# Moving the premix of the next group behind scores and the product with v, and a second bank for the last product with v

## The chip, the cores and the metric

The kernel runs on one core of a Trainium2 chip. It is one program of 22852 instructions on five queues: TensorE (matmuls, PE in the profile, with its weight loads as PEld), VectorE (DVE), ScalarE (ACT), GpSimd (POOL) and SyncE (SP), which here only starts DMA transfers. The metric is the device time of one execution in microseconds (us). Three runs of the kernel before took 1380.95, 1381.3 and 1382.7 us; the median is 1381.3 us.

## The reference

The program is an attention layer whose heads are mixed before and after the softmax, followed by two feed-forward layers. All of it is float32.

```python
def _attn_ref(q, k, v, w_pre, w_post):            # q, k, v: 4 x 12 x 448 x 64
    scores = scale * np.matmul(q, k.transpose(0, 1, 3, 2))
    scores = np.einsum('bhij,hg->bgij', scores, w_pre)      # premix of the 12 heads
    scores = scores - np.max(scores, axis=-1, keepdims=True)
    attn = np.exp(scores)
    attn = attn / (np.sum(attn, axis=-1, keepdims=True) + 1e-09)
    attn = np.einsum('bhij,hg->bgij', attn, w_post)         # postmix
    return np.matmul(attn, v)

def _moe_ref(x, w1, w2, w3, w_out):               # x: 1792 x 768
    return ((x @ w1) * (x @ w2) @ w3) @ w_out

def _moe2_ref(x, w_in, w_out):
    h = x @ w_in
    return np.maximum(0.01 * h, h) @ w_out
```

## The kernel before, in words

The attention part takes the first third of the time, the feed-forward part the rest. Only the attention part is touched.

**Tiling.** Each of the 4 batches is cut into four chunks of query rows: three of 120 rows (`c` = 0, 1, 2) and one of 88 (`c` = 3). A chunk's scores (`qk`, line 199) go through PSUM into a tile `s`, from there by DMA to DRAM (`sdr`), and come back (`relayout`, line 243) as `sr` with the heads of ten query rows on the partitions: that is a block. Two blocks make a group. A chunk of 120 rows has six groups, the one of 88 rows five, and the last of these five holds only one block.

**One step of the loop** (line 421) works on several groups at once. In step `k`:

1. `softmax(groups[k])`: VectorE finds the row maximum `mx` from the premixed scores in PSUM (line 276), ScalarE computes `e` = exp and the sum `sm` (line 279). First block A, then block B.
2. `postmix(groups[k - 1])`: TensorE multiplies `e` of the group before by its weights `kr` (line 304), and VectorE or ScalarE copies the result out of PSUM into `ap` (line 311). Between the blocks stands `weigh(groups[k])`: GpSimd adds a small number to `sm` (line 286), VectorE takes the reciprocal `rc` (line 288), GpSimd scales the weights to `kr` (line 290).
3. `premix(k + 1)`: TensorE mixes the heads of the next group's scores into two PSUM banks `pm` (line 269), one for each block.
4. `qk`: scores of a chunk two ahead, one pair of heads a step, into two banks `pq`; the last two pairs of a chunk may share a step.
5. `av`: the product with v for the chunk before, `px` (line 324). In the first step of a chunk there is none, in the second there are two, then one a step (two in the third step of a chunk with five groups). After the third and the sixth, VectorE copies `px` to `y` (line 333).
6. Small work that the list `lows` and the generator `filler` hold: the copy of `px`, splits of q and k into two parts of float32r (lines 79 and 179; that of k for the next batch stands in the last two steps of `c` = 1 and the first four of `c` = 2), and a piece of the conversion of a feed-forward weight (lines 95 to 106), one a step and two in the third step of a chunk.

**What sets the order.** Within attention the order is written by hand: every engine's queue runs the instructions in the order in which the code above issues them. The feed-forward part behind it is ordered by a scheduler when the program is built. PSUM has eight banks: two `qa` (for `pq`), three `pm`, two `po`, one `px`. A tile takes the bank that its tag hands round, and waits until the last reader of that bank is done. With three `pm` banks, block B of group k + 1 takes the bank in which block A of group k stood, so its premix waits for the exp of that block.

**The way into the feed-forward part.** Behind the loop stand the six products with v of the last chunk. The first feed-forward matmuls (`pw`, line 517) need the first tile of a converted weight `ws`: a DMA brings `wr`, ScalarE takes the absolute value (line 95), VectorE works on it in four instructions (lines 97, 100, 103, 106), ScalarE and VectorE split the result into `ws` (lines 76 and 79).

Of the kernel before, what the change touches and what calls it, by code (L numbers as in the profile page):

```python
# [23 lines left out]
def attention_moe_kernel(ctx: ExitStack, tc, qt, kt, vt, w_pre, w_post, w1, w2, w3t, w_out, w_in2, w_out2, out):  # L24
# [15 lines left out]
    P = 128  # L40
# [5 lines left out]
    CH = qt.shape[-1]  # L46
# [25 lines left out]
    def bank(tag, shape, name):  # L72
        return ps.tile(shape, F32, tag=tag, name=name, bufs=banks[tag])
# [45 lines left out]
    def attention():  # L119
        with ExitStack() as es:  # L120
# [70 lines left out]
            def q_split(b, c):  # L191
                m = cols[c]
                qs = kv.tile([P, NPAIR, 2, CH], F32R, tag="qs", name="qs", bufs=2)
                t = qls.pop((b, c))
                qst[b, c] = qs
                hi_act(qs[:, :, 0, :m], t[:, :, :m])
                return lambda: lo_dve(qs[:, :, 1, :m], t[:, :, :m], qs[:, :, 0, :m])
# [35 lines left out]
            def evict():  # L233
                while evs:
                    evs.pop(0)()

            def flush():

                while stores:
                    dst, t = stores.pop(0)  # L240
                    nc.sync.dma_start(out=dst, in_=t)  # L241
# [20 lines left out]
            def premix(k):  # L262

                sr = srt.pop(k)
                for s, n in enumerate(groups[k]):
                    pms[n] = bank("pm", [P, S], "pm")
                    rows = slice(s * Q, s * Q + blocks[n][3] // 2 * H)
                    for g in range(2):
                        nc.tensor.matmul(  # L269
                            pms[n][g * Q:(g + 1) * Q], kpre[rows], sr[rows, g, :], start=True, stop=True  # L270
                        )

            def softmax(n):
                pm = pms.pop(n)
                mx = wk.tile([P, 1], F32, tag="mx", name="mx")
                nc.vector.tensor_reduce(out=mx, in_=pm, axis=AX.X, op=ALU.max, negate=True)  # L276
                e = wk.tile([P, S], F32, tag="e", name="e", bufs=4)
                sm = wk.tile([P, 1], F32, tag="sm", name="sm")
                ends["act"] = nc.scalar.activation(  # L279
                    out=e, in_=pm, func=ACTF.Exp, bias=mx, scale=1.0, accum_out=sm  # L280
                )
                ets[n], sms[n] = e, sm
# [30 lines left out]
            def av(b, c, p):  # L313
                c0, ni, _ = chunks[c]
                ap = apt[b, c]
                g, r = divmod(p, 3)
                if p == 0:
                    ys[b, c] = yp.tile([P, NPAIR, CH], F32, tag="y", name="y")
                if r == 0:
                    pxs[0] = bank("px", [P, 3, CH], "px")  # L320
                y, px = ys[b, c], pxs[0]
                for jc in range(NJ):
                    for e in range(2):
                        nc.tensor.matmul(  # L324
                            px[e * D:(e + 1) * D, r, :ni],
                            vst[b][:, jc, 2 * p + e, :],
                            ap[:, jc, 2 * p + e, :ni],
                            start=(jc == 0),
                            stop=(jc == NJ - 1),
                        )  # L330
                if r == 2:
                    copy = nc.scalar.copy if (b, c) == order[-1] else nc.vector.tensor_copy
                    lows.append(lambda: copy(y[:, 3 * g:3 * g + 3, :ni], px[:, :, :ni]))
                if p == NPAIR - 1:
                    later.append((scr[b][:, :, c0:c0 + ni], y[:, :, :ni]))

            pxs, later = [None], []
# [40 lines left out]
            order = [(b, c) for b in range(B) for c in range(len(chunks))]  # L378
# [6 lines left out]
            NG = len(groups)  # L385
# [35 lines left out]
            for k in range(NG + 1):  # L421
                flush()
                while later:
                    stores.append(later.pop(0))
                evict()
                if k < NG:
                    b, c, t, nt = where[k]
                    ci = order.index((b, c))
                    for n in groups[k]:
                        softmax(n)  # L430
                for i in range(2):
                    if k > 0 and i < len(groups[k - 1]):
                        postmix(groups[k - 1][i], nc.scalar.copy if i and (k == NG or t % 2) else nc.vector.tensor_copy)
                    if k < NG and i < len(groups[k]):
                        weigh(groups[k][i])
                if k + 1 < NG:
                    premix(k + 1)
                if k < NG:
                    if k + AHEAD < NG:
                        relayout(k + AHEAD)  # L440
                    if ci + QAHEAD < len(order):
                        ps = [t] if nt == NPAIR else [4, 5] if t == 4 else [t]
                        if ci == 0:
                            ps = ([], [0], [1], [2], [3], [4, 5])[t]
                        for p in ps:
                            qk(*order[ci + QAHEAD], p)
                    left = nt - t if t else 1
                    for _ in range(-(-len(todo) // left)):
                        av(*todo.pop(0))
                    if t == 0 and k > 0:  # L450
                        todo += [(*where[k - 1][:2], p) for p in range(NPAIR)]
                    if ci + QAHEAD + 1 < len(order) and t == (4 if ci == 0 or c == NC - 2 else 3):
                        lows.append(q_split(*order[ci + QAHEAD + 1]))
                    if b + 1 < B:
                        if c == NC - 3 and t >= 4:
                            lows.append(k_split(b + 1, t - 4))
                        if c == NC - 2 and t < 4:
                            lows.append(k_split(b + 1, t + 2))
                while lows:
                    lows.pop(0)()  # L460
                if k < NG:
                    if c == 0 and t == 2:
                        v_prep(b)
                    if (t == 4 or k == 0) and ci + QAHEAD + (1 if k == 0 else 2) < len(order):
                        q_load(*order[ci + QAHEAD + (1 if k == 0 else 2)])
                    if b + 1 < B and c == NC - 3 and t in (0, 1, 3):
                        k_load(b + 1, (0, 1, 3).index(t))
                    if k >= START or k == START - 5:
                        for _ in range(2 if k >= START and t == 2 else 1):
                            next(filler, None)  # L470
# [242 lines left out]
```

## Time and profile before

| | |
|---|---|
| median of three runs | 1381.3 us |
| profiled execution | 1380.92 us, span 1379.1 us |
| PE busy | 1335.9 us (97% of the span) |
| DVE busy | 879.3 us (64%) |
| ACT busy | 601.9 us (44%) |
| POOL busy | 166.2 us (12%) |
| DMA queue of SyncE | 222.73 MB, 51.9% of 16 engines' span |
| chain that ended last | PE 90%, DMA 3%, DVE 2%, SPq 2%, ACT 1% |
| first `pw` that runs without a pause | 492.54 us; from there 886.6 us to the end of the span |

Some 1.8 us of the execution lie outside the span. A matmul's end in the profile is modelled, so an engine can stand as busy although the second half of a premix waits inside such a stretch; the starts of the pieces behind each other show the wait better than the busy time. The profile counts two records for each float32 matmul, so a premix of two blocks is x8 and a postmix of two blocks x16. "Releaser" names what ended a wait.

### The profile page before, as it was taken

The page shows a single profiled execution, that of the slowest core. Times are in us where ns is not written, and L with a number is a line of the kernel's source. Part 1 is how long each engine was busy: PE and PEld are TensorE (multiplying, and loading weights), DVE is VectorE, ACT ScalarE, POOL GpSimd, SP SyncE. Part 2 cuts the span into 40 slices and gives each one's busy share as a digit, 9 for nine tenths or more (in the row PEclk, how much of TensorE's full clock was granted, in tenths as well). Part 3 has the DMA queues.
Part 4 walks back from the last instruction along what each step waited for, and adds up shares of the span by engine and source line. Part 5 has one row for each costly group of instructions (what it writes and reads, how often), then busy time and mean ns, then how long its engine had stood idle before and what let it go on. Part 6 is the DMA issues. An engine that isn't in the chain of part 4 may idle for free.

```text
span 1379.1 us, 22852 instructions
## 1 busy us (share of the span) xinstructions
PE 1335.9 (97%) x8880; PEld 1128.7 (82%) x8880; DVE 879.3 (64%) x1519; ACT 601.9 (44%) x1163; POOL 166.2 (12%) x371
## 2 busy tenths in 40 slices
PE   5899999999999989999999999999999999999998
PEld 3466666666666679999898999999898989999998
DVE  4366566566566687576347696967665358596862
ACT  4366566556564354333224452443333225453340
POOL 1233333334333300000000000000000000000000
PEclk8799999999999999999999999999999999999999
DMA  5987897797697796433133432427332233342402
GB/s 170 262 292 207 246 308 234 230 313 236 206 281 250 230 294 208 132 93 91 46 119 109 139 115 92 137 90 226 104 111 66 70 115 111 121 135 93 137 1 80
DMA packets 138859, 224.18 MB, mean 163 GB/s; under 512 B 20032, under 2 KB 120384, under 8 KB 138304
## 3 DMA queue, kind: packets, MB, share of 16 engines
q1 hardware_dynamic: 138752, 222.73, 51.9%
q8 instruction: 70, 1.15, 0.3%
q14 instruction: 37, 0.30, 0.1%
HBM read 162.86 MB, written 58.98 MB: 161 GB/s over the span
## 4 chain that ended last, share of the span: by engine, by line
PE 90%; DMA 3%; DVE 2%; SPq 2%; ACT 1%; issue 1%; POOL 1%; ACTq 0%; POOLq 0%; DVEq 0%
PE pm L579 42%; PE po L648 17%; PE po L304 9%; PE pm L269 6%; PE px L324 5%; PE pq L215 5%; PE pw L517 5%; DMA sr<-sdr 1%; SPq L260 1%; ACT e L279 1%; POOL kr L290 1%; DMA wr<-in_moe_w_dram 1%; DVE mx L276 0%; SPq L241 0%; DMA kl<-in_k_dram 0%
## 5 line engine op out<-in xcount | busy, mean ns | idle before, releaser
L579 PE MATMUL pm<-x,ws 128*128 128x512 f32 (+1 forms) x2304 | 466.8, 363 | 0.0
L579 PEld LDWEIGHTS pm<-x,ws 128*128 128x128 f32 x2304 | 417.7, 188 | 47.7
L648 PE MATMUL po<-ws,g 128*128 128x384 f32 x1344 | 234.2, 334 | 0.0
L648 PEld LDWEIGHTS po<-ws,g 128*128 128x128 f32 x1344 | 233.1, 188 | 0.0
L304 PE MATMUL po<-kr,e 128*112 128x120 f32 (+1 forms) x1440 | 176.1, 275 | 2.5 <-POOL kr L290 2.4
L304 PEld LDWEIGHTS po<-kr,e 128*112 128x112 f32 x1440 | 157.2, 179 | 23.4 <-issue 9.7
L79 DVE TENSOR_TENSOR ws<-wc,ws 128x768 fp32r<-128x768 f32 (+1 forms) x104 | 101.3, 976 | 81.5 <-ACT ws L76 81.2
L279 ACT ACTIVATE e<-pm,mx 128x448 f32<-128x448 f32 x180 | 112.6, 632 | 91.1 <-DVE mx L276 90.7
L95 ACT ACTIVATE wc<-wr 128x768 f32<-128x768 f32 (+2 forms) x120 | 104.6, 874 | 82.9 <-DVE ws L79 61.4
L76 ACT ACTIVATE ws<-wc 128x768 fp32r<-128x768 f32 (+1 forms) x104 | 89.1, 859 | 107.4 <-PE po L648 73.9
L269 PE MATMUL pm<-sr,kpre 60*64 60x448 f32 x720 | 119.4, 572 | 17.0 <-DMA sr<-s 6.9
L290 POOL TENSOR_SCALAR kr<-kpost,rc 128x120 f32<-128x120 f32 x180 | 122.9, 683 | 95.9 <-DVE rc L288 43.9
L223 ACT ACTIVATE s<-pq 120x448 f32<-120x448 f32 (+1 forms) x180 | 88.5, 540 | 101.5 <-PE pq L215 101.3
L579 PE MATMUL pm<-h,ws 128*128 128x512 f32 (+1 forms) x576 | 116.3, 363 | 0.0
L276 DVE TENSOR_REDUCE mx<-pm 128x1 f32<-128x448 f32 x180 | 103.9, 617 | 18.5 <-PE pm L269 18.4
L311 DVE COPY ap<-po 112x480 f32<-112x480 f32 (+1 forms) x136 | 88.4, 650 | 41.0 <-PE po L304 38.2
L579 PEld LDWEIGHTS pm<-h,ws 128*128 128x128 f32 x576 | 104.3, 188 | 11.7
L215 PEld LDWEIGHTS pq<-ks,qs 64*120 64x120 f32 (+1 forms) x576 | 48.4, 184 | 76.5 <-issue 55.0
L106 DVE SCALAR_TENSOR_TENSOR wc<-wr,wc 128x768 uint32<-128x768 uint32 (+2 forms) x120 | 110.0, 917 | 1.3
L103 DVE SCALAR_TENSOR_TENSOR wc<-wr,wc 128x768 uint32<-128x768 uint32 (+2 forms) x120 | 109.9, 917 | 1.2
L324 PEld LDWEIGHTS px<-ap,vs 112*64 112x64 f32 x1536 | 74.0, 136 | 31.9 <-issue 24.5
L215 PE MATMUL pq<-ks,qs 64*120 64x448 f32 (+1 forms) x576 | 89.4, 414 | 10.3 <-ACT ks L76 5.8
(51 smaller groups left out, 992.1 us busy)
## 6 DMA issues: line engine op xcount, KB each, us to landing
sr<-sdr SPq DMA_DIRECT2D x172, 210.0 KB
sdr<-s SPq DMA_DIRECT2D x36, 840.0 KB
wr<-in_moe_w_dram SPq DMA_DIRECT2D x32, 768.0 KB
wr<-in_moe_w_in_dram SPq DMA_DIRECT2D x32, 768.0 KB
wr<-in_moe_w_out_dram SPq DMA_DIRECT2D x32, 768.0 KB
wr<-in_moe_w_dram SPq DMA_DIRECT2D x8, 1024.0 KB
sdr<-s SPq DMA_DIRECT2D x12, 616.0 KB
wr<-in_moe_w_out_dram SPq DMA_DIRECT2D x16, 384.0 KB
```

What stands on the lines that cost most here:

```text
L95: nc.scalar.activation(out=cf, in_=hi.bitcast(F32), func=ACTF.Abs)
L103: lambda: nc.vector.scalar_tensor_tensor(out=c, in0=hi, scalar=0xC0000000, in1=c, op0=ALU.bitwise_and, op1=ALU.bitwise_or),
L106: lambda: nc.vector.scalar_tensor_tensor(out=c, in0=lo, scalar=29, in1=c, op0=ALU.logical_shift_right, op1=ALU.bitwise_or),
L215: nc.tensor.matmul(pq[e][:m], qst[b, c][rows, p, x, :m], kst[b, p][rows, y, :], start=(j == 0), stop=(j == 2))
L269: nc.tensor.matmul(pms[n][g * Q:(g + 1) * Q], kpre[rows], sr[rows, g, :], start=True, stop=True)
L276: nc.vector.tensor_reduce(out=mx, in_=pm, axis=AX.X, op=ALU.max, negate=True)
L279: ends["act"] = nc.scalar.activation(out=e, in_=pm, func=ACTF.Exp, bias=mx, scale=1.0, accum_out=sm)
L290: ends["pool"] = nc.gpsimd.tensor_scalar(out=kr, in0=kpost, scalar1=rc, scalar2=None, op0=ALU.mult)
L304: nc.tensor.matmul(po[:, jc].rearrange("p h (g i) -> p h g i", g=2), e[:, jc * JP:(jc + 1) * JP], kr, start=True, stop=True,)
L324: nc.tensor.matmul(px[e * D:(e + 1) * D, r, :ni], vst[b][:, jc, 2 * p + e, :], ap[:, jc, 2 * p + e, :ni], start=(jc == 0), stop=(jc == NJ ...
L579: nc.tensor.matmul(dst, wt[:, a, kk, :], x[:, kk, c, c0:c0 + w], start=(kk == 0 and j == 0), stop=(kk == kn - 1 and j == 2),)
L648: nc.tensor.matmul(po, g[:, m, a, t * P:(t + 1) * P], wts[m][:, c, 0, cs], start=(m == 0 and j == 0), stop=(m == FQ - 1 and j == 2),)
```

## The change

The call of `premix(k + 1)` moves from behind the postmix to behind the products with v, at the end of the matmuls of a step. In the last six products with v, the second three go to a bank of `qa` in place of the only `px` bank.

```diff
                 if r == 0:
-                    pxs[0] = bank("px", [P, 3, CH], "px")
+                    pxs[0] = bank("qa" if g and (b, c) == order[-1] else "px", [P, 3, CH], "px")
...
                     if k < NG and i < len(groups[k]):
                         weigh(groups[k][i])
-                if k + 1 < NG:
-                    premix(k + 1)
                 if k < NG:
...
                     if t == 0 and k > 0:
                         todo += [(*where[k - 1][:2], p) for p in range(NPAIR)]
+                    if k + 1 < NG:
+                        premix(k + 1)
                     if ci + QAHEAD + 1 < len(order) and t == (4 if ci == 0 or c == NC - 2 else 3):
```

On TensorE this is the order of one step and the start of the next, at the turn from one chunk to another (the step at the turn has no product with v). Before:

```order
L304 MATMUL po<-kr,e 112x120 x8
L269 MATMUL pm<-sr,kpre 64x448 x4
L215 MATMUL pq<-ks,qs 88x448 x6
L324 MATMUL px<-ap,vs 64x120 x8
L304 MATMUL po<-kr,e 112x120 x8
L269 MATMUL pm<-sr,kpre 64x448 x4
L215 MATMUL pq<-ks,qs 120x448 x6
L304 MATMUL po<-kr,e 112x120 x8
```

And after, at the same place:

```order
L304 MATMUL po<-kr,e 112x120 x8
L215 MATMUL pq<-ks,qs 88x448 x6
L324 MATMUL px<-ap,vs 64x120 x8
L269 MATMUL pm<-sr,kpre 64x448 x4
L304 MATMUL po<-kr,e 112x120 x8
L215 MATMUL pq<-ks,qs 120x448 x6
L269 MATMUL pm<-sr,kpre 64x448 x4
L304 MATMUL po<-kr,e 112x120 x8
```

The premix (L269) has gone from the second place of a step to the last; nothing else has changed places. Within attention VectorE, ScalarE, GpSimd and SyncE keep their order; only a few loads of SyncE for the feed-forward part, near the end of the loop, stand between other loads than before.

The scheduler of the feed-forward part deals out its first instructions anew. On VectorE, right behind the last copy of the loop, `wc_6185` and `ws_6191` belong to the first weight tile, `wc_6196` and `ws_6202` to the second. Before:

```order
L97 TENSOR_SCALAR wc_6185<-wc_6185 128x1024
L100 TENSOR_SCALAR wc_6185<-wc_6185 128x1024
L103 SCALAR_TENSOR_TENSOR wc_6185<-wr_6179,wc_6185 128x1024
L106 SCALAR_TENSOR_TENSOR wc_6185<-wr_6179,wc_6185 128x1024
L97 TENSOR_SCALAR wc_6196<-wc_6196 128x1024
L100 TENSOR_SCALAR wc_6196<-wc_6196 128x1024
L103 SCALAR_TENSOR_TENSOR wc_6196<-wr_6181,wc_6196 128x1024
L79 TENSOR_TENSOR ws_6191<-wc_6185,ws_6191 128x1024
L106 SCALAR_TENSOR_TENSOR wc_6196<-wr_6181,wc_6196 128x1024
```

And after:

```order
L97 TENSOR_SCALAR wc_6185<-wc_6185 128x1024
L100 TENSOR_SCALAR wc_6185<-wc_6185 128x1024
L103 SCALAR_TENSOR_TENSOR wc_6185<-wr_6179,wc_6185 128x1024
L97 TENSOR_SCALAR wc_6196<-wc_6196 128x1024
L106 SCALAR_TENSOR_TENSOR wc_6185<-wr_6179,wc_6185 128x1024
L100 TENSOR_SCALAR wc_6196<-wc_6196 128x1024
L103 SCALAR_TENSOR_TENSOR wc_6196<-wr_6181,wc_6196 128x1024
L106 SCALAR_TENSOR_TENSOR wc_6196<-wr_6181,wc_6196 128x1024
L79 TENSOR_TENSOR ws_6191<-wc_6185,ws_6191 128x1024
```

The whole conversion of the second tile now stands ahead of the last instruction for the first one, and its first instruction ahead of the fourth for the first tile.

On TensorE, `px_6087` and `px_6113` are the two banks of the last six products with v, `pw_6207` and `pw_6235` the halves of the first feed-forward result, `pw_6274` and `pw_6307` those of the second. Before:

```order
L324 MATMUL px_6087<-ap_5898,vs_4955 64x88 x24
L324 MATMUL px_6113<-ap_5898,vs_4955 64x88 x24
L517 MATMUL pw_6207<-wo_6170,ws_6191 128x384 x2
L517 MATMUL pw_6235<-wo_6170,ws_6191 128x384 x2
L517 MATMUL pw_6207<-wo_6170,ws_6191 128x384 x22
L517 MATMUL pw_6235<-wo_6170,ws_6191 128x384 x22
```

And after:

```order
L324 MATMUL px_6087<-ap_5898,vs_4955 64x88 x24
L324 MATMUL px_6113<-ap_5898,vs_4955 64x88 x24
L517 MATMUL pw_6207<-wo_6170,ws_6191 128x384 x2
L517 MATMUL pw_6235<-wo_6170,ws_6191 128x384 x2
L517 MATMUL pw_6274<-wo_6170,ws_6202 128x384 x2
L517 MATMUL pw_6307<-wo_6170,ws_6202 128x384 x2
L517 MATMUL pw_6207<-wo_6170,ws_6191 128x384 x22
```

Four short matmuls on the second tile now come before the long part on the first.

## Rows read from the trace of the kernel before

**Rows 1.** Stretches: us, each engine's busy time (records), granted clock, DMA share, GB/s

```profile
47.50:51.50 4.00, 3.92 (x14) 1.43 (x14) 1.25 (x2) 0.00 (x0) 0.00 (x0) 0.50 1.02 249
...
54.50:479.50 425.00, 412.75 (x4036) 280.85 (x4034) 266.07 (x622) 246.09 (x620) 159.56 (x351) 1.00 0.83 252
```

**Rows 2.** Waits of 54.5 to 479.5 us: engine, tile, releaser: us, times, longest

```profile
PE pm L269 <- ACT e L279: 4.6, 10, 0.7
...
PEld pm L269 <- ACT e L279: 20.1, 25, 1.4
...
PEld po L304 <- POOL kr L290: 6.2, 13, 1.1
```

**Rows 3.** Stretches with premix (line 269) alone: us, PE busy, PEld busy, clock, DMA

```profile
54.50:479.50 425.00, 107.34 (x696) 22.97 (x696) 1.00 0.83 252
```

**Rows 4.** Timeline of PE: start, us, line, tiles, records [wait before, releaser]

```profile
106.99 1.89 PE L304 MATMUL po<-kr,e 128*112 128x120 f32 x16
108.82 0.98 PE L269 MATMUL pm<-sr,kpre 60*64 60x448 f32 x8
109.73 0.87 PE L215 MATMUL pq<-ks,qs 64*120 64x448 f32 x6
110.53 1.04 PE L324 MATMUL px<-ap,vs 112*64 112x120 f32 x16
...
111.50 1.89 PE L304 MATMUL po<-kr,e 128*112 128x120 f32 x16
...
114.95 0.97 PE L269 MATMUL pm<-sr,kpre 60*64 60x448 f32 x4 [0.66 <-ACT e L279]
```

**Rows 5.** Timeline of VectorE before the premix that waits in rows 4

```profile
111.61 0.53 DVE L333 COPY y<-px 128x360 f32<-128x360 f32 x1 [1.52 <-PE px L324]
...
113.46 1.15 DVE L276 TENSOR_REDUCE mx<-pm 128x1 f32<-128x448 f32 x2
```

**Rows 6.** Timeline of VectorE and GpSimd, 126.5 to 132 us: one group's way to kr

```profile
127.67 1.15 DVE L276 TENSOR_REDUCE mx<-pm 128x1 f32<-128x448 f32 x2
...
129.78 0.59 POOL L290 TENSOR_SCALAR kr<-kpost,rc 128x120 f32<-128x120 f32 x1 [0.36 <-DVE rc L288]
...
131.04 0.59 POOL L290 TENSOR_SCALAR kr<-kpost,rc 128x120 f32<-128x120 f32 x1 [0.37 <-PE pq L215]
```

**Rows 7.** Timeline, 97 to 103 us: a group whose second kr is slow

```profile
97.84 1.15 DVE L276 TENSOR_REDUCE mx<-pm 128x1 f32<-128x448 f32 x2
...
100.96 0.62 DVE L179 TENSOR_TENSOR ks<-kl,ks 128x448 fp32r<-128x448 f32 x1
...
101.21 1.22 POOL L290 TENSOR_SCALAR kr<-kpost,rc 128x120 f32<-128x120 f32 x1 [0.36 <-PE pq L215]
```

**Rows 8.** Timeline of PE, steps without scores (445 us)

```profile
445.05 0.98 PE L269 MATMUL pm<-sr,kpre 60*64 60x448 f32 x8
445.96 1.04 PE L324 MATMUL px<-ap,vs 112*64 112x120 f32 x16
```

**Rows 9.** Timeline of PE at the start of the loop

```profile
47.58 2.65 PE L269 MATMUL pm<-sr,kpre 60*64 60x448 f32 x8 [5.41 <-DMA sr<-sdr]
50.16 1.47 PE L215 MATMUL pq<-ks,qs 64*120 64x448 f32 x6
51.56 3.05 PE L304 MATMUL po<-kr,e 128*112 128x120 f32 x16
```

**Rows 10.** Way into the feed-forward part: timeline, then the chain that ended last

```profile
486.67 1.15 ACT L95 ACTIVATE wc<-wr 128x1024 f32<-128x1024 f32 x1 [1.62 <-DMA wr<-in_moe_w_dram]
487.53 1.22 DVE L106 SCALAR_TENSOR_TENSOR wc<-wr,wc 128x1024 uint32<-128x1024 uint32 x1
...
489.39 0.69 DVE L100 TENSOR_SCALAR wc<-wc 128x1024 uint32<-128x1024 uint32 x1
...
489.90 0.96 PE L517 MATMUL pw<-wo,ws 128*128 128x384 f32 x4 [2.75 <-ACT ws L76]
...
492.54 68.49 PE pw L517 x380
```

## The prediction

> **What bounds the kernel now.** I read the stretches of the span first. From 54.5 to 479.5 us, the loop of the attention part, TensorE is busy 412.75 of 425.00 us at a granted clock of 1.00 (of 2.4 GHz), VectorE 266.07 us, and the 16 DMA engines are 0.83 busy [rows 1]. So TensorE sets the pace, and a change of order can give back only what TensorE stands still, which is hidden in part in stretches that count as busy. The waits say for what: the weight load of the premix waits 25 times for ScalarE's exp, 20.1 us in all, its matmuls stand idle for 4.6 us, and the weight loads of the postmix wait 13 times for `kr`, 6.2 us [rows 2]. The timeline gives the size of an undisturbed step, read from start to start: postmix 1.83, premix 0.91, scores 0.80, product with v 0.97, together 4.51 us [rows 4]. The first step of a chunk has no product with v (3.53), one without scores and product 2.73.
>
> **Why the premix waits.** The bank of its second block is free when the first exp of the step is done, and that exp waits for `mx` on VectorE. In a step behind a copy of `px`, VectorE comes to `mx` late: the copy starts at 111.61, right behind the product with v, and with the small work behind it `mx` starts at 113.46, 1.96 us into the step that began at 111.50 [rows 4, 5]. The second half of the premix then starts at 114.95 where 113.33 would have done.
>
> **The change part by part.**
>
> *The waits for the bank go.* The stretch of the loop holds 696 records of premix; that is 174 blocks in 89 premixes, of which four have one block. An undisturbed one is busy 0.98 us [rows 4], 89 of them 87.2; they are busy 107.34 [rows 3], so 20.1 us of waiting stand as busy, and 4.6 us as waits [rows 2]: 24.7 us. After the change the premix starts 0.80 to 2.6 us later in its step, at least 1.75 us behind the end of the premix before, and the bank is free 1.5 us behind `mx` (113.46 to 114.95 [rows 4, 5]). No bank is late unless `mx` is 0.25 us behind the premix in the shortest step, or 2.1 us in an ordinary one. Gain: 24.7; what a late bank would cost stands in the rivals.
>
> *The old waits for `kr` go, and others come.* Of the 6.2 us in rows 2 TensorE loses 4.3: so much are the postmixes of the loop over 1.83 each from start to start on the timeline. These waits hang on the old place of `mx`. In their place: from now on `mx` cannot start before the premix that ends a step. Call that end T. What is queued behind `mx` on VectorE (copies of `po`, reciprocals, the small work) all shifts with it, and the next postmix waits for the `kr` made from it. From `mx` to the end of the first `kr` is 127.67 to 130.37, 2.70 us, to the end of the second 131.63, 3.96 us [rows 6]. With VectorE's subtraction for k beside it the second `kr` takes 1.22 in place of 0.59, and the way 97.84 to 102.43, 4.59 us [rows 7]. I add 0.05 to the start of the postmix and see where that is later than TensorE:
>
> - An ordinary step: block A is wanted at T + 4.51, B at T + 5.42. `mx` at T + 0.11 (as the copy of `px` behind its product [rows 4, 5]) gives 2.86 and 4.12, slow 4.75. No wait.
> - Fourth steps of `c` = 2, behind copy, subtraction and two pieces of conversion: in rows 5 these take 1.85 from the copy to `mx`; the copy starts 0.11 behind the product, which now ends 0.91 before T, so `mx` is at T + 1.05 and B ready at 5.69: wait 0.27. Three times: 0.8.
> - Second steps of `c` = 2 wait for a group whose `mx` stood behind copy, subtraction and one piece (1.85 less 0.38): `mx` at T + 0.67, B ready at 5.31, wanted at 3.53 + 0.91 = 4.44: 0.87. Three times: 2.6.
> - Behind the group of one block the postmix is 0.95, so that step is only 2.66 long: A waits 0.2 and B 0.35. Three times: 1.7.
> - First steps without scores (2.73): 0.15 and 0.35. Twice: 1.0.
> - The third step of the last chunk has two products with a copy between them; VectorE reaches that copy some 0.4 later, behind the reciprocals: 0.4.
>
> New waits: 6.5. The undisturbed steps keep their time, since the four pieces are the same; on ScalarE the scores' copies now come 0.9 earlier and stand out of exp's way. Two waits stay as they are: the second of two score pairs in one step, and the product behind a copy.
>
> *The start of the loop.* The premix of 47.58 waits 5.41 us for a transfer; the scores behind it (50.16 to 51.56) move into this wait [rows 9]. That saves 1.40, at a granted clock of 0.50 [rows 1]. But the clock then has the same time to rise in as before, so the next scores may still run at the low one, 1.40 for 0.80. Gain between 0.8 and 1.4; I take 1.0.
>
> *The last product.* The wait for `px` goes, but behind it TensorE waits 2.75 us, until 489.90, for the first `ws` [rows 10]: 0, since the weight stays the later one; a part of 2.75 only if the weight came sooner. The loop's last piece of conversion, the store and loads behind it move up with the loop, so I let the entry shift with it.
>
> *The first feed-forward weight.* Line 97 for the second tile now stands ahead of line 106 for the first and waits for an absolute value that ends at 487.82, where VectorE was free at 487.53. From there line 97 takes 0.69 (as line 100), line 106 1.22; then lines 100, 103 and 106 for the second tile take 0.69, 1.22 and 1.22 (line 103 as line 106), and ScalarE's split for the short matmuls 1.15 (487.53 + 1.22 to 489.90): TensorE starts its unbroken run at about 494.0 rather than 492.54 [rows 10]. Bounds: 0 if the scheduler's order costs nothing, 2.5 if the subtraction for the first tile also stands in the way. I take 1.4, since these instructions overlap a little. From there to the end TensorE has no pause worth naming in both orders.
>
> Sum, from the profiled 1380.92: - 24.7 - 4.3 + 6.5 - 1.0 + 1.4 = **1358.8, say 1359 us**. The median of the runs shown is 0.4 above that execution, which changes nothing.
>
> **Two rules weighed.** The slow `kr` of rows 7 runs beside an instruction of VectorE with two operands from SBUF. The Trainium skill, "SBUF — State Buffer", section "Who interferes with whom", says that such an instruction and one of GpSimd that reads SBUF block each other for the whole instruction, whichever issues first. The trace agrees in kind: 1.22 against 0.59. By the rule the slow `kr` comes back wherever that subtraction is queued behind the reciprocal; were it 0.59 throughout, the waits at `c` = 2 would be 0.75 and 0 in place of 2.6 and 0.8, and the sum 1356.
>
> TensorE gets new neighbours: premix ahead of postmix, product ahead of premix. A premix takes 0.91 to the next start ahead of scores and ahead of a product with v alike [rows 4, 8]. "TensorEngine Tiling (Array Packing)" of the Trainium skill, section "Key Properties", says that each change of the tiling mode drains the engine. The number of such changes in a step is the same, so by the rule the sum stays; that some pair costs more than another no run here shows, and it is the second rival.
>
> **Rivals.**
>
> - *Fewer new waits.* VectorE's small work finds room, and the 6.5 do not come, with the start at 1.4 and the entry at 0: 1380.92 - 29.0 - 1.4 = 1350.5; half of it, 1354. For it: VectorE is busy 63% of the loop [rows 1]. Against it: its order is fixed, and the way from `mx` to `kr` is as long as before. 10%.
> - *New neighbours on TensorE cost time.* The nearest price is one weight load of a postmix, about 0.11 us (1.83 for 16 records); exposed once in each of 89 steps that is 9.8: 1368.6. The same length could as well be saved, below 0. Against it: the equal 0.91 above. 12%.
> - *Transfers come late.* The loop shortens by 22 us and the DMA share rises from 0.83 to 0.87 [rows 1]; two waits like the 5.41 at the start would bring 1370. Against it: the premix now stands later in its step, and past 54.5 no premix waits for a transfer. 4%.
> - *Slower: the way from premix to `kr` sets every step.* Premix, `mx`, exp, reciprocal, `kr`, postmix follow each other with nothing in reserve but one step. If `mx` were late by 1.05 and the second `kr` slow everywhere, some 60 ordinary steps would wait 0.27 (16) and 15 first steps 1.25 (19): 35 for 6.5, 1387. It decides against the change from about 29 us of such waits, that is from a mean lateness of `mx` of about 1 us. For it: VectorE now stands idle at the head of each step. Against it: only two steps in a chunk have the copy, one has two pieces, and the subtraction stands in six of 23 steps. 8%, of which 3% between 1378 and 1384.
>
> **How the numbers follow.** The forecast has 66%, its own range 1353 to 1366. The range 1350 to 1371 adds most of the first three rivals and leaves out the slower case and the rest. A measurement of this kernel can tell about 0.2% (2.8 us) from no change. Faster by over 0.2%: 0.66 + 0.10 + 0.12 + 0.04 less a little, 0.91. Within: 0.03. Slower: 0.06.
>
> **What would show it.** In the changed profile the wait of the premix for exp should be gone from 25 places; VectorE should wait for the premix ahead of `mx` in most steps; the waits of the postmix for `kr` should be 5 to 8 us and stand in second steps; an ordinary step should stay at 4.51; the run of `pw` should start 20 to 22 us earlier, at 470 to 473, and last as long as before. The prediction is wrong if an ordinary step is over 4.6, if postmix waits for `kr` in fourth and fifth steps throughout, or if the premix waits for `sr`.

## The result and the profile after

The changed kernel takes 1358.05 us (median of four, 1357.54 to 1358.5); the one before, run beside it, 1381.24. The ratio is 0.983, with a 95% interval of 0.9813 to 0.9847. The forecast was 1359, its range 1350 to 1371. The profiled span went from 1379.1 to 1356.7 us.

**Where the time went.** Two postmixes serve as marks in both kernels: the third of the loop and the last, which holds one block. From mark to mark each piece is measured from its start to the next start. The undisturbed lengths are 1.82 for a postmix (0.91 for one block), 0.91 for a premix and 0.76 to 1.79 for one or two products; what goes beyond them by more than 0.06 is added up as late. The last postmix, which lies outside the loop, is counted in with 0.75 in both.

| us | before | after | change | predicted |
|---|---|---|---|---|
| start of the span to the third postmix | 56.26 | 54.84 | -1.42 | -1.0 |
| premixes late | 25.44 (25 places) | 1.34 (5) | -24.10 | -24.7 |
| postmixes late | 5.06 | 6.75 | +1.69 | +1.8 |
| products late | 3.42 | 3.96 | +0.54 | +0.4 |
| third to last postmix | 423.31 | 401.54 | -21.77 | -22.5 |
| last postmix to the unbroken `pw` | 12.97 | 13.38 | +0.41 | +1.4 |
| from there to the end of the span | 886.56 | 886.94 | +0.38 | 0 |

The stretches of the span after, with the columns of [rows 1]; the third is the loop between the same times of the program:

```profile
47.50:51.50 4.00, 3.78 (x15) 1.99 (x16) 1.25 (x2) 1.18 (x3) 0.22 (x1) 0.50 1.01 265
51.50:54.50 3.00, 3.00 (x25) 2.19 (x24) 1.55 (x4) 0.74 (x4) 1.03 (x3) 0.82 1.12 255
54.50:457.00 402.50, 393.43 (x4034) 276.53 (x4027) 267.07 (x621) 243.64 (x620) 158.43 (x349) 1.00 0.87 268
```

The same loop, line 269 alone, with the columns of [rows 3]:

```profile
54.50:457.00 402.50, 87.01 (x696) 18.41 (x688) 1.00 0.87 268
```

The 89 premixes are busy 87.01 us where they were 107.34 [rows 3]; 89 undisturbed ones were reckoned at 87.2. All the waiting that stood as busy is gone. The DMA share rose to the 0.87 foreseen, without a late transfer. The waits of that stretch, with the columns of [rows 2]:

```profile
DVE mx L276 <- PE pm L269: 35.6, 35, 2.1
PEld po L304 <- POOL kr L290: 32.4, 49, 1.1
...
PE px L324 <- DVE y L333: 2.9, 4, 1.0
PE po L304 <- POOL kr L290: 2.9, 10, 0.5
```

No row "pm <- ACT e" is left. In its place VectorE waits for the premix. The second row is to be read with care: the weight loads of the postmix wait 32.4 us for `kr`, five times the 6.2 of [rows 2], but the postmixes are late by only 1.7 more in all. A weight load now gets to its wait while the premix ahead of it is still running, and only what outlasts that premix costs time. TensorE's timeline shows it (columns of [rows 4]):

```profile
97.89 1.07 PE L304 MATMUL po<-kr,e 128*112 128x120 f32 x8
99.17 1.07 PE L304 MATMUL po<-kr,e 128*112 128x120 f32 x8 [0.21 <-POOL kr L290]
100.18 0.88 PE L215 MATMUL pq<-ks,qs 64*120 64x448 f32 x6
...
103.69 1.89 PE L304 MATMUL po<-kr,e 128*112 128x120 f32 x16
105.51 0.86 PE L215 MATMUL pq<-ks,qs 64*120 64x448 f32 x6
106.30 1.04 PE L324 MATMUL px<-ap,vs 112*64 112x120 f32 x16
107.27 0.98 PE L269 MATMUL pm<-sr,kpre 60*64 60x448 f32 x8
108.19 1.89 PE L304 MATMUL po<-kr,e 128*112 128x120 f32 x16
...
112.70 2.23 PE L304 MATMUL po<-kr,e 128*112 128x120 f32 x16
114.86 0.87 PE L215 MATMUL pq<-ks,qs 64*120 64x448 f32 x6
```

The step of 103.69 takes 1.82 + 0.79 + 0.97 + 0.92 = 4.50, as before. The second step of the chunk (97.89) has 0.47 more in its postmix, the fifth (112.70 to 114.86) 0.34 more. The `kr` that the fifth step waits for comes from the `mx` of the fourth step, which starts at 108.19. VectorE between the product of 106.30 and that `mx` (columns of [rows 5]):

```profile
107.39 0.53 DVE L333 COPY y<-px 128x360 f32<-128x360 f32 x1 [0.39 <-PE px L324]
107.84 0.62 DVE L179 TENSOR_TENSOR ks<-kl,ks 128x448 fp32r<-128x448 f32 x1
...
108.76 0.56 DVE L103 SCALAR_TENSOR_TENSOR wc<-wr,wc 128x384 uint32<-128x384 uint32 x1
109.23 1.15 DVE L276 TENSOR_REDUCE mx<-pm 128x1 f32<-128x448 f32 x2
```

The premix ends at 108.19 and `mx` starts 1.04 later; the forecast said 1.05.

The start of the loop on TensorE, to be held against [rows 9]:

```profile
41.99 1.00 PE L215 MATMUL pq<-ks,qs 64*120 64x448 f32 x6
47.72 2.50 PE L269 MATMUL pm<-sr,kpre 60*64 60x448 f32 x8 [4.72 <-DMA sr<-sdr]
50.15 3.05 PE L304 MATMUL po<-kr,e 128*112 128x120 f32 x16
53.13 0.87 PE L215 MATMUL pq<-ks,qs 64*120 64x448 f32 x6
```

The scores now stand ahead of the wait for the transfer, and the next ones (53.13) already take 0.80 to the following start. That was not so in every execution. move_only, a kernel of the experiments below, has the same order on TensorE up to here; its granted clock was 0.50 until 53.7 us, in the changed kernel until 52.6, and its postmix and its next scores took longer:

```profile
49.76 3.54 PE L304 MATMUL po<-kr,e 128*112 128x120 f32 x16
53.23 1.07 PE L215 MATMUL pq<-ks,qs 64*120 64x448 f32 x6
```

Now the way into the feed-forward part, on three engines, and the first `pw` without a pause in the chain that ended last (compare [rows 10]):

```profile
459.42 1.17 ACT L95 ACTIVATE wc<-wr 128x1024 f32<-128x1024 f32 x1 [4.35 <-DMA wr<-in_moe_w_dram]
...
462.44 1.13 ACT L95 ACTIVATE wc<-wr 128x1024 f32<-128x1024 f32 x1 [1.85 <-DMA wr<-in_moe_w_dram]
463.61 0.69 DVE L97 TENSOR_SCALAR wc<-wc 128x1024 f32<-128x1024 f32 x1 [0.30 <-ACT wc L95]
464.21 1.22 DVE L106 SCALAR_TENSOR_TENSOR wc<-wr,wc 128x1024 uint32<-128x1024 uint32 x1
...
468.48 2.49 DVE L79 TENSOR_TENSOR ws<-wc,ws 128x1024 fp32r<-128x1024 f32 x2
```

```profile
469.76 68.92 PE pw L517 x380
```

Line 97 for the second tile (463.61) waits 0.30 and pushes line 106 for the first to 464.21, as the forecast said. The long run then waits for two results that come within 0.02 us of each other: the first tile's subtraction (L79, 468.48 and 1.22 long) and ScalarE's split of the second tile for the short matmuls, through which the chain that ended last goes. The first weight's absolute value starts 3.04 us behind the last postmix (456.38), where it was 4.09 behind the one of 479.57. Its piece of the chain before:

```profile
483.66 1.13 ACT wc L95
```

From that start to the unbroken `pw` it is 10.34 us, where it was 8.88.

### The profile page after: what moved, and what is told of

It is laid out like the page before. It is cut to its first block, busy times and chain, and to the rows that moved or that the text cites. A ratio compares the mean times of both kernels' runs of the same rounds, so it can differ in the third digit from the quotient of the medians.

```text
span 1356.7 us, 22900 instructions
## 1 busy us (share of the span) xinstructions
PE 1317.7 (97%) x8880; PEld 1125.8 (83%) x8880; DVE 881.0 (65%) x1519; ACT 601.0 (44%) x1163; POOL 166.0 (12%) x371
## 4 chain that ended last, share of the span: by engine, by line
PE 89%; DMA 3%; DVE 2%; SPq 2%; POOL 2%; ACT 2%; issue 1%; POOLq 0%; ACTq 0%; DVEq 0%
PE pm L579 43%; PE po L648 17%; PE po L304 9%; PE px L324 5%; PE pw L517 5%; PE pm L269 5%; PE pq L215 4%; POOL kr L290 1%; SPq L260 1%; ACT e L279 1%; DMA sr<-sdr 1%; DMA wr<-in_moe_w_dram 1%; DMA sdr<-s 1%; DVE mx L276 1%; SPq L241 0%
## 5 line engine op out<-in xcount | busy, mean ns | idle before, releaser
L304 PEld LDWEIGHTS po<-kr,e 128*112 128x112 f32 x1440 | 157.3, 179 | 72.0 <-POOL kr L290 32.4
L79 DVE TENSOR_TENSOR ws<-wc,ws 128x768 fp32r<-128x768 f32 (+1 forms) x104 | 101.6, 978 | 81.6 <-ACT ws L76 81.2
L76 ACT ACTIVATE ws<-wc 128x768 fp32r<-128x768 f32 (+1 forms) x104 | 89.3, 861 | 110.1 <-PE po L648 74.0
L269 PE MATMUL pm<-sr,kpre 60*64 60x448 f32 x720 | 99.1, 571 | 11.4 <-DMA sr<-s 6.6
L97 DVE TENSOR_SCALAR wc<-wc 128x768 f32<-128x768 f32 (+2 forms) x120 | 64.9, 541 | 50.1 <-ACT wc L95 49.9
L324 PE MATMUL px<-ap,vs 112*64 112x120 f32 (+1 forms) x1536 | 90.4, 264 | 3.6 <-DVE y L333 2.9
```

The costliest lines, as they stand in the source:

```text
L269: nc.tensor.matmul(pms[n][g * Q:(g + 1) * Q], kpre[rows], sr[rows, g, :], start=True, stop=True)
L304: nc.tensor.matmul(po[:, jc].rearrange("p h (g i) -> p h g i", g=2), e[:, jc * JP:(jc + 1) * JP], kr, start=True, stop=True,)
L324: nc.tensor.matmul(px[e * D:(e + 1) * D, r, :ni], vst[b][:, jc, 2 * p + e, :], ap[:, jc, 2 * p + e, :ni], start=(jc == 0), stop=(jc == NJ ...
```

## The experiments

Times are medians. The ratio is to the kernel before, run beside them on the same chip (medians of 1380.98, 1381.3 and 1380.95 us); old_pm2 and new_late have a single run each. "Loop" is from the third to the last postmix, "entry" from the last postmix to the unbroken `pw`, "late" as above; these columns are from one profiled execution of each kernel. What precedes the third postmix differs from execution to execution (55.2 to 57.0 us with the premix in its old place, 52.6 to 55.1 in the new one), and the entry from kernel to kernel with the order that the scheduler happens to deal out. So the loop column is the one to compare.

| kernel | us | ratio, interval | loop | premix late | postmix late | entry |
|---|---|---|---|---|---|---|
| before | 1381.2 | 1 | 423.31 | 25.44 | 5.06 | 12.97 |
| the change | 1358.05 | 0.983 (0.9813 to 0.9847) | 401.54 | 1.34 | 6.75 | 13.38 |
| move_only | 1358.25 | 0.9836 (0.9822 to 0.9849) | 401.59 | 1.37 | 6.76 | 13.00 |
| bank_only | 1378.78 | 0.9984 (0.9975 to 0.9993) | 423.28 | 25.42 | 5.07 | 10.83 |
| old_defer | 1353.09 | 0.9796 (0.9781 to 0.9811) | 395.82 | 0.00 | 3.06 | 12.79 |
| new_defer | 1356.02 | 0.982 (0.9807 to 0.9834) | 400.10 | 1.01 | 5.35 | 13.23 |
| old_pm2 | 1404.19 | one run | 448.70 | 23.81 | 32.47 | 10.56 |
| new_pm2 | 1353.28 | 0.9795 (0.9782 to 0.9808) | 397.71 | 2.41 | 5.64 | 12.44 |
| new_late | 1374.51 | one run | 421.31 | 7.00 | 19.46 | 12.49 |
| entry2 | 1353.45 | 0.9796 (0.9783 to 0.9809) | 401.56 | 1.39 | 6.64 | 9.49 |
| best_a | 1350.34 | 0.9784 (0.977 to 0.9797) | 395.78 | 0.00 | 3.06 | 11.13 |
| best_b | 1350.87 | 0.9787 (0.9774 to 0.9801) | 397.78 | 2.55 | 5.51 | 11.08 |
| best_c | 1358.63 | 0.9838 (0.9824 to 0.9851) | 403.32 | 10.61 | 3.32 | 10.64 |
| best_d | 1347.43 | 0.976 (0.9747 to 0.9773) | 395.11 | 2.27 | 3.29 | 9.48 |

### Each part alone

move_only is the changed kernel without the second bank; bank_only is the kernel before with it.

```diff
-                    pxs[0] = bank("qa" if g and (b, c) == order[-1] else "px", [P, 3, CH], "px")
+                    pxs[0] = bank("px", [P, 3, CH], "px")
```

> The changed kernel, but the last product with v keeps its one px bank: only the premix has moved. Theory (the move frees the premix from waiting for exp, and the second bank hides nothing): 1358 us, as the changed kernel, within 1 us; premix waits in the loop about 1.5 us in place of 25.5, and the first unbroken pw starts within 0.3 us of that of the changed kernel (13.4 us behind the last postmix). Rival (the second bank brings part of the gain): 1359.5 to 1361.

> The kernel before, but the last three products with v take a bank of qa; the premix stays in its old place. Theory (the second bank hides nothing): 1379.5 to 1382, with the old 25 waits of the premix for exp; only the order of the first feed-forward weights on VectorE differs by one instruction, worth about 1.2 us. Rival (the second bank brings part of the gain): 1378 or less.

The move is the whole of the gain. With one bank TensorE waits again in front of the last three products (timeline of move_only):

```profile
464.50 3.79 PE L324 MATMUL px<-ap,vs 112*64 112x88 f32 x48 [4.06 <-ACT y L333]
```

Even so the unbroken `pw` starts 13.00 us behind the last postmix with this wait and 13.38 without it. But that is not because the weight is late whatever the bank does. The chain that ended last in move_only goes through the bank: from those products to the copy of `px` on ScalarE, and from there to the split of the first weight, which stands behind that copy in ScalarE's queue:

```profile
468.34 0.02 ACT y L333
...
468.62 1.07 ACT ws L76
...
469.73 68.58 PE pw L517 x384
```

In the changed kernel that split (L76) starts 9.08 us behind the last postmix, in move_only 11.89. So two waits stand beside each other there, the one for the bank and the one for VectorE. In both kernels VectorE has the first tile's subtraction (L79) behind the whole conversion of the second tile, and starts it 12.09 us behind the last postmix even where the bank is free. Taking the one wait away leaves the other. Whether the second bank is worth something once the conversions stand in turn was not run. bank_only missed its expectation by 0.7 us. Its loop is that of before to 0.03 us; what it gains lies in the entry, 2.1 us shorter. The scheduler deals out the weight conversion differently there (6.29 us from the first absolute value to the unbroken `pw`, where it was 8.88), which led to entry2.

### Another cure for the same wait

If the premix waited because `mx` came late, then VectorE can do `mx` sooner and the premix stay where it was. old_defer is the kernel before with VectorE's small work put behind `mx` and the first reciprocal; new_defer is the same edit in the changed kernel.

```diff
+            def settle():
+                while lows:
+                    lows.pop(0)()
...
                     if k < NG and i < len(groups[k]):
                         weigh(groups[k][i])
+                    if i == 0:
+                        settle()
...
                     for _ in range(-(-len(todo) // left)):
+                        settle()
                         av(*todo.pop(0))
...
-                while lows:
-                    lows.pop(0)()
+                if k >= NG - 1:
+                    settle()
```

> The kernel before, with the premix in its old place, but VectorE does the small work at a step's end (copy of px, subtractions for q and k) only behind the row maxima and the first reciprocal of the next step, so that mx is not late. Theory (the premix waited because mx stood behind that work): 1358 to 1363 us; the 25 waits of the premix for exp fall to under 5 us. Rival (the old place itself makes the premix wait, whatever VectorE does first): 1375 to 1382.

> The changed kernel, with VectorE's small work put behind the row maxima and the first reciprocal of the next step. Theory (the 6.5 us that the postmix still waits for kr come from a late mx in some steps, and in part from a slow kr beside the subtraction for k): 1355 to 1357.5 us, postmix waits 3 to 5 us. Rival (they come from the length of the way from premix to kr alone): no change, 1358.

Both theories came out against their rivals, and old_defer went past its range: 1353.09, faster than the change itself. VectorE's timeline in it, at the step that answers to [rows 5] (it starts at 108.28) and the next one (112.79):

```profile
107.96 1.14 DVE L276 TENSOR_REDUCE mx<-pm 128x1 f32<-128x448 f32 x2
...
110.04 0.51 DVE L333 COPY y<-px 128x360 f32<-128x360 f32 x1
110.47 0.66 DVE L179 TENSOR_TENSOR ks<-kl,ks 128x448 fp32r<-128x448 f32 x1
111.24 0.16 DVE L288 RECIPROCAL rc<-sm 128x1 f32<-128x1 f32 x1
111.32 0.54 DVE L106 SCALAR_TENSOR_TENSOR wc<-wr,wc 128x384 uint32<-128x384 uint32 x1
111.78 1.15 DVE L276 TENSOR_REDUCE mx<-pm 128x1 f32<-128x448 f32 x2
```

Copy and subtraction now stand behind `mx` and fill VectorE's pause ahead of the second reciprocal. `mx` starts 0.32 ahead of its step, where it was 1.96 behind the start, and the next one 1.01 ahead of its own. No premix is late any more. Postmixes are late by 3.06, less than the 5.06 of before, since an earlier `mx` makes `kr` earlier too; in the new place `mx` cannot go ahead of the premix, and new_defer keeps 5.35 + 1.01.

### How many premix banks the two places need

```diff
-    banks = {"qa": 2, "pm": 3, "po": 2, "px": 1}
+    banks = {"qa": 2, "pm": 2, "po": 2, "px": 2}
```

old_pm2 has this in the kernel before, new_pm2 in the changed one, both with all products in the two `px` banks.

> The kernel before with two pm banks in place of three, and the bank that becomes free given to px. Theory (in its old place the premix stands right behind exp, and needs the third bank): both blocks of the premix wait for both exps, 1393 to 1402 us, premix waits 40 us or more in the loop. Rival (the third bank plays no part): 1378, the gain of the second px bank (3.4 us) alone.

> The changed kernel with two pm banks in place of three, and the bank that becomes free given to px throughout (the last product too). Theory (at a step's end the exps of the group before have been done for 1 us and more, so two banks do, but for the shortest steps, 3 to 4 us): 1355 to 1358.5 us, with the product's 3.9 us of waits for the px copy gone. Rival (the premix needs three banks wherever it stands): 1365 or more.

The waits of 54.5 to 450 us in old_pm2, and those in new_pm2:

```profile
PEld pm L269 <- ACT e L279: 41.0, 61, 1.8
PE pm L269 <- ACT e L279: 22.3, 24, 1.6
```

```profile
PEld pm L269 <- ACT e L279: 4.2, 14, 0.4
```

With one bank less the old place loses 25.4 us in the loop, and its 1404.19 lies above the 1402 expected. Not all of this is waiting. The 32.47 that the table gives as postmixes late are for the most part the pause in front of the premix behind them, since its first block now waits for exp as well. And in five stretches of the loop, 17 us together, the granted clock is 0.50, which no other kernel has there; each begins less than 1 us behind a premix in front of which TensorE had stood still for 0.96 to 1.56 us, though other pauses as long have none behind them. The first of them (the premix with its wait, then the stretch with the columns of [rows 1]):

```profile
118.58 1.58 PE L269 MATMUL pm<-sr,kpre 60*64 60x448 f32 x8 [1.56 <-ACT e L279]
```

```profile
120.14:123.56 3.42, 3.42 (x25) 2.51 (x24) 2.21 (x5) 1.96 (x5) 1.42 (x2) 0.50 0.09 23
```

The postmixes, scores and products in these stretches took some 8 us more than undisturbed ones. So about 17 of the 25.4 are waits for the bank, and 8 came through the clock. The new place loses 1.1 in its premixes and more than makes up for it, since the bank moved to `px` takes away 3.8 of the 3.96 that products waited behind a copy of `px`, and the postmixes are late by 1.1 less. So the place of the premix was worth a bank. The gain of new_pm2 beside the change, 4.8, is also more than was expected; 3.8 of it lies in the loop, 0.9 in the entry.

### How much reserve the new order has

new_late adds a needless VectorE reduction of `pm`, of one block, ahead of every `mx` from the third step on. It tests the slower rival, the way from premix to `kr`.

```diff
+                    if k > 1:
+                        nc.vector.tensor_reduce(out=idle, in_=pms[groups[k][0]], axis=AX.X, op=ALU.max)
                     for n in groups[k]:
                         softmax(n)
```

> The changed kernel with one more row reduction of VectorE (0.58 us) between the premix and mx in each step from the third on; nothing of the output depends on it. Theory (an ordinary step has about 1.3 us in reserve on the way from mx to kr, only first steps have 0.3): the postmix waits some 10 us more, 1364 to 1372. Rival (the way from premix to kr sets every step): 0.58 in each of 89 steps, about 1409.

The loop grew by 19.8 us, twice what my theory expected (1374.51 lies outside its 1364 to 1372) and two fifths of the 51 by which the rival's 1409 would have come. 37 postmixes and 13 premixes are late. VectorE at the fourth step of the same chunk, and the postmix behind it on TensorE:

```profile
111.28 0.62 DVE L431 TENSOR_REDUCE idle<-pm 128x1 f32<-128x448 f32 x1
111.82 0.61 DVE L277 TENSOR_REDUCE mx<-pm 128x1 f32<-128x448 f32 x1
```

```profile
114.65 1.07 PE L305 MATMUL po<-kr,e 128*112 128x120 f32 x8
116.46 1.07 PE L305 MATMUL po<-kr,e 128*112 128x120 f32 x8 [0.74 <-POOL kr L291]
```

The premix ended at 110.14 and `mx` starts 1.68 later; the second block of the postmix is 0.9 late. These are waits for `kr`: for exp the weight loads of the premix wait 0.6 us in all (54.5 to 450 us). One instruction of 0.54 more on VectorE takes nearly all that the move gave (21.8), so the new order is near its limit.

### The order of the first two weight conversions

entry2 is the changed kernel, with the second tile's conversion bound to begin behind the last instruction for the first.

```diff
-        nc.vector.tensor_tensor(out=dst, in0=src, in1=hi.bitcast(F32), op=ALU.subtract)
+        los.append(nc.vector.tensor_tensor(out=dst, in0=src, in1=hi.bitcast(F32), op=ALU.subtract))
...
-                        wt = next_w()
+                        wt = next_w(2 if f else 1)
+                    if f == 0:
+                        ends["first"] = los[-1]
```

> The changed kernel, with the first feed-forward weight converted and split to its end before VectorE begins with the second. Theory (the new order of the conversions costs 1.4 us at the entry): the first unbroken pw starts about 2.9 us earlier behind the last postmix than in the changed kernel, of which the second weight may take back up to 2: 1355 to 1357.5 us. Rival (TensorE waits for the transfer, not for the order on VectorE): 1358.

Its timeline, at the place of the rows above:

```profile
459.06 1.17 ACT L95 ACTIVATE wc<-wr 128x1024 f32<-128x1024 f32 x1 [4.53 <-DMA wr<-in_moe_w_dram]
...
462.98 1.22 DVE L106 SCALAR_TENSOR_TENSOR wc<-wr,wc 128x1024 uint32<-128x1024 uint32 x1
464.24 1.06 ACT L76 ACTIVATE ws<-wc 128x1024 fp32r<-128x1024 f32 x1 [0.48 <-DVE wc L106]
465.33 1.22 DVE L79 TENSOR_TENSOR ws<-wc,ws 128x1024 fp32r<-128x1024 f32 x1 [1.12 <-ACT ws L76]
```

From the absolute value to the unbroken `pw` (465.35) it is 6.29 us in place of 10.34, and the kernel gains 4.6, more than expected; in the profiled execution 3.9 lie in the entry, and some 0.5 each in the start and behind the entry. The subtraction for the first tile (L79) came at 468.48 in the changed kernel, behind lines 100, 103 and 106 for the second: the scheduler's order puts the first weight last. The kernel before paid part of that price as well (8.88).

### Versions put together

best_a is old_defer with entry2's edit, best_b is new_pm2 with it, best_c is best_a with the two banks of old_pm2, best_d is best_b with the small work behind the maximum.

> The premix in its old place, three premix banks, VectorE's small work behind the maximum, and the first feed-forward weight converted before the second. If the two edits act in different stretches, their gains add: from 1353.1 us (the old place with the small work behind the maximum) the 4.6 us that the entry's order brought beside the change: 1348.5 us, within 1. Rival: the entry's order repairs only what the move of the premix had put there (the first weight's arrival); then little is left to gain in the old place and it stays above 1351.

> The premix in the new place with two premix banks and two of the product with v, and the entry's order. The gains of the two runs that had one edit each add: 1353.3 - 4.6 = 1348.7 us, within 1. Rival: with two premix banks the loop's end leaves VectorE busier when the feed-forward begins, and the entry gives less than half of its 4.6: above 1351.

> The premix in its old place, the small work behind the maximum, but only two premix banks and two of the product with v, and the entry's order. If lateness of VectorE's maximum was all that the third premix bank covered, the two banks do and the px waits (3.4 us) go: about 1345 us. If the old place needs a third bank because the bank's exponential cannot be done one step earlier, premix waits of some 20 to 45 us come back as they did with two banks without the deferral: 1365 to 1390. I take the second, about 1370.

> The premix in the new place, two premix banks and two of the product with v, the small work behind the maximum, and the entry's order: the three gains that were measured apart beside the change (2.0, 4.8 and 4.6 us) add to 1346.6 us if each removes other waits. If the small work and the banks remove the same waits (those of the postmix for the ready sums), 1348 to 1349, as without the small work's move.

The entry's edit leaves the loop alone: the loops of best_a and best_b are those of old_defer and new_pm2 within 0.1 us. The entry's gain did not come in full; it is 1.7 and 1.4 us in place of 3.9. There are two reasons. The first is that less was left to gain: from the first absolute value to the unbroken `pw` it was 8.88 us in old_defer and 8.95 in new_pm2, not 10.34, and it is 6.56 and 6.93 with the edit. So best_a's rival was right in part: 1.46 of the price had come with the move. The second is that the absolute value starts later behind the last postmix, 4.57 and 4.15 where it was 3.92 and 3.50 (3.19 in best_d). Its load stands on SyncE behind a load of `wo`, which in the changed kernel's chain waits for the store of the loop's last piece of conversion (`wos`). From the issue of that store to that of the load it is 4.50 and 4.14 us in best_a and best_b, 3.78 and 3.14 in old_defer and new_pm2. Why the store takes longer in one execution than in another was not settled.

best_c was faster than I took it, and slower than if two banks were enough. Its waits of 54.5 to 450 us:

```profile
PEld pm L269 <- ACT e L279: 7.6, 22, 0.6
```

The premix waits are back in 25 places, but none is over 0.55 us. Against best_a its loop has 10.6 more of them, 0.3 more in the postmixes and 3.4 less of product waits, together the 7.5 by which it is longer. So lateness of `mx` explains most, not all, of what the third bank does in the old place.

best_d, with the premix at the step's end, two banks each for it and for the product, VectorE's small work behind `mx` and the conversions in turn, takes 1347.43 us, 0.976 of the kernel before (0.9747 to 0.9773). Its interval lies wholly below that of the change, and touches best_a's. The time lies between the two that were expected, 1346.6 and 1348. Its loop is 6.4 us shorter than that of the change, where the small work (1.4) and the banks (3.8) took 5.3 apart: in the loop the two do not remove the same waits.

## Why the prediction was right

- **The bank.** The 24.7 us were read from two views that had to be added: 4.6 of waits, and 20.1 that stood as busy. The 25.44 by which premixes were late are gone; the 1.34 that stand there now are waits for `kr`, below. That lateness of `mx` was the cause is shown by old_defer, which takes these waits away without touching TensorE's order. new_late makes `mx` late with the move made, and then the waits that come are those for `kr`, not those for the bank.
- **The waits for `kr`.** The old ones were 4.31 (5.06 less 0.75), as read. After the change there are 6.00 in postmixes and 1.34 behind premixes, 7.3 in place of 6.1: this term was sized too low. Second steps of `c` = 2 cost 0.47, 0.74 and 0.47 in place of 0.87 each; the late `mx` of fourth steps 0.34, 0 and 0.35 in the postmix behind it, for 0.27 each; behind groups of one block 0.70 on the mean for 0.55; first steps without scores 0.82 and 1.14 for 0.5. One wait of 0.54 the forecast did not have: in a fifth step of `c` = 1 (postmix of 191.19) the second `kr` takes 1.62 beside VectorE's subtraction for q, which starts at 190.74. The errors are of both signs, and those of short steps were too low. The wait for a first block shows as a longer premix, since the postmix behind it starts later; that is the 1.34.
- **The start.** 1.42 for 1.0, the upper end of the bounds (1.4), in the two executions compared. That the next scores "may still run at the low" clock did not come true in this one (0.80 for the scores of 53.13), but it did in three of the eight kernels with the premix in its new place: 1.00 in move_only, 1.06 in new_defer and new_pm2. The start differs by over 2 us among kernels with the same order on TensorE, so one pair of executions does not size this term.
- **The second bank.** 0 in sum, as move_only shows, but the reason given, that "the weight stays the later one", is only half of it. In move_only the chain goes through the bank, and the weight's first split waits behind the copy of `px`. The gain is 0 because VectorE's order of the conversions costs as much beside it; that the two waits are about equally long is luck.
- **The entry.** The term for the scheduler's order, 1.4, measured 1.46 (10.34 less 8.88) from the first absolute value on, through the instructions that the forecast named. But the load came 1.05 earlier behind the last postmix, which the forecast did not have ("I let the entry shift with it"): the store of `wos` that it stands behind is issued 8.06 us ahead of the last postmix, where it was 7.02. The sum was +0.41. The +0.38 behind the entry fit the clock, which was granted at 0.50 for the first 6.0 us of the unbroken `pw`, where it was 5.2 us.
- **The sum.** Against the profiled execution (1358.50) the 1358.8 are 0.3 too high. The loop gained 0.7 less than forecast, start and entry came out 0.4 and 1.0 better, the rest 0.4 worse. That these errors cancel is luck; the term that carries the result, 24.7 for 24.10 in the premixes, is not.
- **The rivals.** New neighbours on TensorE cost nothing: all four pieces kept their length within 0.01. No premix of the loop waits for a transfer on TensorE's own rows. The slower rival's point was set too far off: it was to decide from a mean lateness of 1 us, and new_late lost 19.8 us from 0.54 on each step.
- **What it said the profile would show.** Bank waits gone, 4.50 a step, and `kr` waits of 5 to 8 us came true. That VectorE waits for the premix in most steps did not (35 times in 89). The `kr` waits stand in second steps, as it said: 5.9 of the 7.3 us, in nine of these steps (those behind a group of one block and behind a first step without scores among them). The unbroken `pw` started at 469.76, a little ahead of the 470 to 473.

## What to carry to other kernels

When a matmul waits for a PSUM bank, follow the chain that frees the bank back to the engine that is late, and ask first whether that engine has work ahead of it that could wait: here that reordering alone (1353.09) beat the move of the matmul (1358.05). Moving the consumer later gives the chain more room and can be worth a bank, but takes the same room from what hangs behind it; so price the next link at each kind of step, the short ones above all. After any change look at a scheduled part behind it too, since the order of its first instructions was worth 4.6 us here.

## What the runs showed beside this

A wait of weight loads in the list of waits says little by itself: 32.4 us of them stood beside 2.9 us of TensorE's own. And a wait can cost more than its own length: in old_pm2 the granted clock fell to 0.50 five times in the loop, each time behind a premix that TensorE had stood still for, and 8 of the 25.4 us lost came that way.
